# The chunked scan's outputs and states made for two sequences in one group of TensorE products, from the second block on

## The chip, the cores and the metric

One core of a Trainium2 chip. The metric is the device time of one execution in microseconds (us). A core has five engines that run their own instruction lists: PE (TensorE, products), ACT (ScalarE), DVE (VectorE), POOL (GpSimd) and SP (SyncE, which only issues the DMAs here). They wait for one another by semaphores.

## The reference

A gated linear recurrence over 4 sequences of 768 positions, 8 heads, head size 32, state size 16, whose output (3072 tokens of 256 features) goes through two dense networks with 2048 hidden units; float32 throughout.

```python
for c in range(nc):                       # chunks of the sequence
    cum = np.cumsum(log_a[:, :, sl], axis=-1)
    L = np.exp(cum[:, :, :, None] - cum[:, :, None, :]) * causal
    M = np.einsum('bhin,bhjn->bhij', Cc, Bc) * L
    y_intra = np.einsum('bhij,bhjd->bhid', M, xc)
    y_inter = np.einsum('bhin,bhnd->bhid', Cc, state) * np.exp(cum)[:, :, :, None]
    y[:, :, sl] = y_intra + y_inter
    decay_from_j = np.exp(cum[:, :, -1:] - cum)
    Bx = np.einsum('bhjn,bhjd->bhjnd', Bc, xc) * decay_from_j[:, :, :, None, None]
    state = np.exp(np.sum(la, -1))[:, :, None, None] * state + np.sum(Bx, axis=2)
x = y.transpose(0, 2, 1, 3).reshape(3072, 256)
h = x @ moe_w_in
x = (np.maximum(h, 0) + np.log1p(np.exp(-np.abs(h)))) @ moe_w_out
h = x @ moe2_w_in
return np.where(h >= 1, h, np.where(h <= -1, 0, (h + 1) ** 2 / 4)) @ moe2_w_out
```

## The kernel before, in words

The recurrence is cut into blocks of 128 positions: 6 blocks (c) times 4 sequences (b) make 24 units, u = 4c + b. The features of a block, four units side by side, are the 512 tokens of one pass of the dense networks.

Every piece of work is a named job. `program` adds all jobs with an engine, a cost in ns, what they need, the buffers that they take and give back, and for some a due time; `Jobs.order` runs a list scheduler over them once, while the kernel is built, and the code is written out in that order. So each engine's instruction list is fixed by the table of costs and due times, and a change of one job can move others.

The jobs of a unit, in their order:

- `load`, `load_bc` (for two units), `rows`, `dec` (for a block): DMAs that SP issues.
- `decay` (DVE, a scan of 128x1024) makes the decay matrix in a tile `ld`; `cd` (DVE) scales C; `sources` (DVE) scales B.
- `scores` (PE, line 791) makes C times B for two units at once: its four banks of PSUM are the two of the tile `y` (also called `pair`) and two `acc` banks. `weigh` (DVE, line 800, two for a unit) multiplies them into `ld`.
- `out` (PE) makes the unit's features and its state's increment in the tile `y`: 4 products with the old state on 32 rows (line 824), 8 products with x that fill 32 columns each (line 829), and, except in the last block, 4 products for the state (line 836). Each is recorded as two matmuls in the profile.
- `evac` (ACT, line 849) copies the features to `xh`, rounded to the type that PE reads fast; `ready` (DVE, line 858) writes the remainder to `xl`, and for blocks 1 to 4 brings the state `s` forward (line 860). `sm` (ACT) spreads the state for the next block's `out`.

There is one tile `y`, so `out` of a unit waits until `ready` of the unit before it has read it.

The dense networks run in steps: `up` (PE, lines 891 to 893: three products for one of float32, with the high and low parts of features and weights), the nonlinearity `g` (ACT, and DVE in the second network), `g_hi` and `g_lo` (the split of g into high and low part, on ACT, DVE and, for some, POOL, line 930), `down` (PE, line 956). In blocks 0 and 1 a step has 256 tokens (two sequences) and two slices of the hidden size; later it has 512 tokens and one. Weights come as float64 and are turned into a high and a low part by the jobs `w0` to `w3`, `w_hi` and `split_w` on ACT, DVE and POOL.

The tables that matter here, as the scheduler had them: `out` 900 ns (750 in block 0), `evac` 270 ns, `ready` 340 ns, 190 ns more with the state.

Of the kernel before, what the change touches and what calls it, by code (L numbers as in the profile page):

```python
# [12 lines left out]
ALU = mybir.AluOpType  # L13

NB, H, S, D, N = 4, 8, 768, 32, 16
Q = 128
# [154 lines left out]
def place_of(kind, j):  # L171

    return (2 if kind == "i" else 4) + j // 4


def signed(m, kind, j):

    return m == 0 and j < PRELU[kind == "o"]
# [4 lines left out]
    return s < WHOLE  # L183


def on_act(s):

    return NFC * NC <= s < ACT_UNTIL


def program():
# [39 lines left out]
    for u in range(NU):  # L231
# [25 lines left out]
        if b % 2:  # L257
            v = u // 2
            add(
                ("scores", v), PE, 1350, needs=[("load_bc", v)] + (decay + [("decay", u - 1)] if c else [("scores", v - 1)] * v),  # L260
                takes=["y", "acc", "acc"] if c else ["y"] + [("acc", "h")] * 2 if v == 0 else [("h", "acc")] * 4,
                gives=[("load_bc", v)],
            )
        for hg in range(2):
# [10 lines left out]
        needs = [("weigh", u, 0), ("weigh", u, 1)] + ([("out", u - 1)] if u else [])  # L275
        if c > 0:
            needs += [("cd", u), ("sm", u - NB)]
        add(
            ("out", u), PE, 900 if c else 750, needs=needs, takes=["y"],
            gives=[("load", u), ("rows", u) if c else ("part", ("spread", u, 0), 1)] + [("sources", u) if c else ("sources", u, 0)] * (c < NC - 1),  # L280
        )
        needs = [("out", u)]
        if c > 1:
            needs += [("split_w", 0, kind, j) for kind in "io" for j in range(8) if place_of(kind, j) == c]
            needs += [("down", s) for s in range(WHOLE)]
        if c == 1:

            needs += [("w2" if signed(0, kind, SX) else "w3", 0, kind, SX) for kind in "io"]
        due = when(first_step[c, b] - LEAD if c < 2 else min(first_step[c, b] - LEAD, CHUNK * (c - 1) + SPACE * b + SHIFT))
        add(("evac", u), ACT, 270 + 150 * (c == 0), needs=needs)  # L290
        add(
            ("ready", u), DVE, 340 + 190 * (0 < c < NC - 1), due=due, needs=[("evac", u)],
            gives=[("out", u)] + [("dec", c)] * (b == NB - 1 and c > 0),
        )
        if c < NC - 1:
            add(("sm", u), ACT, 500, needs=[("ready", u)] + [("decay", 3, 1)] * (u < NB))


    last_use, first_use = {}, {}
# [26 lines left out]
    for s, (m, c, t0, n, fc, m_fc) in enumerate(steps):  # L326
        pieces = sorted({(fc + i) // 2 for i in range(m_fc)})
        if m == 0:
            needs = [("ready", NB * c + b) for b in range(t0 // Q, (t0 + n) // Q)]
# [96 lines left out]
def tile_kernel(ctx: ExitStack, tc: tile.TileContext, a0, al, bc, ub, w_in, w_out, w2_in, w2_out, out):  # L426
# [380 lines left out]

    emit["copy"] = copy_scores

    def y_t():  # L810

        buf("y", 0)
        return bufs["pair"][:, :, 0:Q], bufs["pair"][:, 0, Q:Q + 64]

    def out_unit(engine, u):
        c, b = divmod(u, NB)
        (y, state), ld = y_t(), ld_t(u)
        x, _, cdt = parts(u)

        if c > 0:  # L820
            for p in range(4):

                r, o = slice(p * 32, p * 32 + 32), p % 2 * 64
                nc.tensor.matmul(  # L824
                    y[o:o + 64, p // 2], sm_t[b][r], cdt[r], start=True, stop=False, skip_group_check=True,
                )
        for h in range(H):
            r = slice(h % 4 * 32, h % 4 * 32 + 32)
            nc.tensor.matmul(  # L829
                y[r, h // 4], x[:, h * 32:h * 32 + 32], ld[:, h, :], start=(c == 0), stop=True, skip_group_check=True,  # L830
            )
        if c < NC - 1:
            bt = flat(bt_t(u))
            for p in range(4):
                r = slice(p * 32, p * 32 + 32)
                nc.tensor.matmul(
                    state[r], bt[:, p * 32:p * 32 + 32], x[:, p * 64:p * 64 + 64], start=False, stop=True,
                    skip_group_check=True,
                )

    emit["out"] = out_unit

    @job
    def evac(engine, u):
        c, b = divmod(u, NB)
        y, state = y_t()
        if b == 0:
            xh[c], xl[c] = (new(f"x{i}{c}", F32R, f"x{i}{c}") for i in "hl")
        nc.scalar.copy(xh[c][:, :, b * Q:(b + 1) * Q], y)  # L849
        if c == 0:  # L850
            nc.scalar.copy(s_t[b], state)

    @job
    def ready(engine, u):
        c, b = divmod(u, NB)
        y, state = y_t()
        hi, lo = (t[:, :, b * Q:(b + 1) * Q] for t in (xh[c], xl[c]))
        nc.vector.tensor_tensor(out=lo, in0=y, in1=hi.bitcast(F32), op=ALU.subtract)  # L858
        if 0 < c < NC - 1:
            nc.vector.scalar_tensor_tensor(  # L860
                out=s_t[b], in0=s_t[b], scalar=mine("dec", c)[0][:, b, Q - 1:Q], in1=state,
                op0=ALU.mult, op1=ALU.add,
            )

    @job
# [220 lines left out]
```

## Time and profile before

| | |
|---|---|
| median of 3 runs | 597.13 us (596.39 to 599.62) |
| the profiled execution | 597.06 us |
| its span, first to last instruction | 595.3 us |
| PE busy | 583.7 us, 98% of the span |
| DVE busy | 469.2 us, 79% |
| ACT busy | 258.6 us, 43% |
| POOL busy | 38.0 us, 6% |
| TensorE's mean granted clock | 1.000 |

A busy engine had an instruction in it; PE's are pipelined, so that its busy share says little of the pace. The pace is read from the starts of successive products.

### The profile page before, as it was taken

To read this page: it belongs to the slowest core of one execution; us is meant where nothing else is said; L and a number is where in the kernel's file an instruction comes from. 1 tells how busy PE (TensorE), PEld (TensorE's weight loads), DVE (VectorE), ACT (ScalarE), POOL (GpSimd) and SP (SyncE) were. 2 spreads that over 40 slices of the span, in tenths; PEclk is the share of its full clock that TensorE was granted. 3 is DMA by queue.
4 is the path that set the end of the run, shared out by engine and by line. 5 is a ranking of instruction groups with operands and counts; after the bars stand their busy time and mean duration, and the time that the engine had idled before them with its cause. 6 is when DMAs were issued, how large, how long until landed. Compare 5 with 4: busy or idle time off the path is not lost.

```text
span 595.3 us, 9221 instructions
## 1 busy us (share of the span) xinstructions
PE 583.7 (98%) x3598; PEld 482.6 (81%) x3598; DVE 469.2 (79%) x789; ACT 258.6 (43%) x469; POOL 38.0 (6%) x28
## 2 busy tenths in 40 slices
PE   7799999999999999999999999999999999999997
PEld 3699989997787778778888888888888888888886
DVE  6899996886756763558998766679899899899895
ACT  5957453443433332236655876653222322322321
POOL 4285300000000000000000000000000000000000
PEclk9999999999999999999999999999999999999999
DMA  7986342522420320005430000000000000000000
GB/s 269 398 303 200 115 138 80 199 90 79 134 70 28 107 72 0 1 1 178 141 107 0 1 1 2 0 35 2 37 0 1 35 2 0 36 0 2 35 1 36
DMA packets 19863, 43.68 MB, mean 73 GB/s; under 512 B 1740, under 2 KB 2316, under 8 KB 19820
## 3 DMA queue, kind: packets, MB, share of 16 engines
q1 hardware_dynamic: 19820, 43.10, 21.2%
q8 instruction: 28, 0.46, 0.3%
q14 instruction: 15, 0.12, 0.1%
HBM read 39.75 MB, written 3.34 MB: 72 GB/s over the span
## 4 chain that ended last, share of the span: by engine, by line
PE 94%; POOL 1%; ACT 1%; DMA 1%; DVE 1%; issue 1%; SPq 0%; ACTq 0%
PE acc L956 43%; PE h L891 11%; PE h L893 10%; PE h L892 10%; PE y L829 2%; PE acc L891 2%; PE acc L892 2%; PE acc L893 2%; PE z L892 2%; PE z L893 2%; PE z L891 2%; PE acc L944 2%; PE y L791 2%; POOL gl L930 1%; PE y L824 1%; DMA st<-in_w_in_dram 1%
## 5 line engine op out<-in xcount | busy, mean ns | idle before, releaser
L956 PE MATMUL acc<-gh,woh 128*128 128x512 f32 (+1 forms) x424 | 152.4, 367 | 0.0
L956 PE MATMUL acc<-gh,wol 128*128 128x512 f32 (+1 forms) x424 | 150.6, 363 | 0.0
L930 DVE TENSOR_TENSOR gl<-g,gh 128x512 fp32r<-128x512 f32 x182 | 125.9, 692 | 21.7 <-ACT gh L501 10.8
L891 PE MATMUL h<-xh,wih 128*128 128x512 f32 (+1 forms) x332 | 120.3, 362 | 0.5 <-ACT xh L849 0.5
L893 PE MATMUL h<-xl,wih 128*128 128x512 f32 (+1 forms) x332 | 118.2, 356 | 0.0
L892 PE MATMUL h<-xh,wil 128*128 128x512 f32 (+1 forms) x332 | 118.1, 356 | 0.0
L956 PE MATMUL acc<-gl,woh 128*128 128x512 f32 (+1 forms) x424 | 115.5, 363 | 0.8 <-POOL gl L930 0.8
L503 DVE CAST gh<-g 128x512 fp32r<-128x512 f32 x121 | 52.6, 435 | 52.1 <-ACT g L915 43.6
L956 PEld LDWEIGHTS acc<-gh,woh 128*128 128x128 f32 x424 | 79.9, 188 | 14.8 <-issue 0.9
L956 PEld LDWEIGHTS acc<-gh,wol 128*128 128x128 f32 x424 | 80.0, 189 | 12.2
L902 ACT ACTIVATE t<-h 128x512 f32<-128x512 f32 x63 | 37.7, 599 | 112.1 <-PE h L893 112.1
L956 PEld LDWEIGHTS acc<-gl,woh 128*128 128x128 f32 x424 | 74.4, 189 | 13.6 <-POOL gl L930 1.0
L891 PEld LDWEIGHTS h<-xh,wih 128*128 128x128 f32 x332 | 62.6, 189 | 12.4 <-issue 2.2
L893 PEld LDWEIGHTS h<-xl,wih 128*128 128x128 f32 x332 | 62.6, 189 | 9.1 <-DVE xl L858 0.2
L892 PEld LDWEIGHTS h<-xh,wil 128*128 128x128 f32 x332 | 62.7, 189 | 8.7
L915 ACT ACTIVATE g<-h 128x512 f32<-128x512 f32 x55 | 32.9, 597 | 74.8 <-PE h L893 67.4
L921 DVE SCALAR_TENSOR_TENSOR t<-t 128x512 f32<-128x512 f32 x72 | 49.6, 690 | 6.0 <-ACT t L902 5.8
L501 ACT CAST gh<-g 128x512 fp32r<-128x512 f32 x65 | 40.4, 621 | 21.9 <-DVE g L922 16.8
L755 DVE TENSOR_TENSOR_SCAN ld<-ld,eye_t 128x1024 f32<-128x1024 f32 x20 | 45.5, 2281 | 0.2 <-DMA ld<-clip_z 0.2
L922 DVE TENSOR_TENSOR g<-h,t 128x512 f32<-128x512 f32 x63 | 43.5, 691 | 2.2
L915 ACT ACTIVATE g<-acc 128x512 f32<-128x512 f32 x27 | 16.1, 598 | 36.1 <-PE acc L893 36.0
L891 PE MATMUL acc<-xh,wih 128*128 128x512 f32 (+1 forms) x66 | 23.2, 352 | 0.0
(147 smaller groups left out, 660.5 us busy)
## 6 DMA issues: line engine op xcount, KB each, us to landing
ld<-clip_z SPq DMA_DIRECT2D x20, 512.0 KB, 4.2
st<-in_w_in_dram SPq DMA_DIRECT2D x15, 512.0 KB, 6.9
st<-in_w_out_dram SPq DMA_DIRECT2D x15, 512.0 KB, 5.1
u<-in_ub_dram SPq DMA_DIRECT2D x24, 256.0 KB, 3.7
bc<-in_bc_dram SPq DMA_DIRECT2D x12, 384.0 KB, 3.5
out_dram<-dec SPq DMA_DIRECT2D x6, 256.0 KB, 3.0
dec<-clip_p SPq DMA_DIRECT2D x5, 256.0 KB
out_dram<-bc SPq DMA_DIRECT2D x5, 256.0 KB, 2.2
```

The lines of the kernel that those rows point to most:

```text
L501: nc.scalar.copy(out, in_)
L503: engines[engine].tensor_copy(out, in_)
L755: nc.vector.tensor_tensor_scan(t, t, eye_t, 0.0, ALU.mult, ALU.add)
L891: nc.tensor.matmul(o, wh, xh[c][:, k, t0:t0 + n], start=(k == 0), stop=False)
L892: nc.tensor.matmul(o, wl, xh[c][:, k, t0:t0 + n], start=False, stop=False)
L893: nc.tensor.matmul(o, wh, xl[c][:, k, t0:t0 + n], start=False, stop=(k == 1))
L902: nc.scalar.activation(out=t, in_=ph, func=AF.Relu, bias=0.5, scale=0.5)
L915: nc.scalar.activation(out=g, in_=ph, func=AF.Softplus)
L921: nc.vector.scalar_tensor_tensor(out=t, in0=t, scalar=1.0, in1=t, op0=ALU.min, op1=ALU.mult)
L922: nc.vector.tensor_tensor(out=g, in0=ph, in1=t, op=ALU.max)
L930: engines[engine].tensor_tensor(out=mine("g_lo", s)[0], in0=mine("g", s)[0], in1=mine("g_hi", s)[0].bitcast(F32), op=ALU.subtract)
L956: nc.tensor.matmul(acc_t(s, e), w, g[:, j * n:(j + 1) * n], start=(begins(e, j) and g is gh and i == 0), stop=(fc + j == NFC - 1 and g is ...
```

## The change

In block 0 nothing changes in the jobs. From block 1 on `out`, `evac` and `ready` are made for two sequences at a time, at the odd unit: `out` puts the 8 products of both with the old state first, then the 16 with x, then the 8 for the states. The features of the two lie side by side in the tile `y` (columns 0 to 127 and 128 to 255 of each bank, the states' increments behind them), one `evac` copies 2x256 columns, one `ready` subtracts 2x256 columns and then brings both states forward with an instruction each. `ready_of` names the job that a later job waits for. The scheduler's costs are: `out` 2200 ns for the pair, `evac` 490, `ready` 610 and 380 more with the states, `scores` 1270 where it was 1350.

```diff
+def ready_of(u):
+
+    return u if u < NB else u | 1
...
-                ("scores", v), PE, 1350, needs=[("load_bc", v)] + (decay + [("decay", u - 1)] if c else [("scores", v - 1)] * v),
+                ("scores", v), PE, 1270, needs=[("load_bc", v)] + (decay + [("decay", u - 1)] if c else [("scores", v - 1)] * v),
...
+        both = [u] if c == 0 else [u - 1, u]
+        if c == 0 or b % 2:
+
+            needs = [("weigh", i, hg) for i in both for hg in range(2)] + ([("out", both[0] - 1)] if u else [])
+            if c > 0:
+                needs += [(kind, i - NB * (kind == "sm")) for i in both for kind in ("cd", "sm")]
+            add(
+                ("out", u), PE, 2200 if c else 750, needs=needs, takes=["y"],
...
+            add(("evac", u), ACT, 490 if c else 420, needs=needs)
+            add(
+                ("ready", u), DVE, 610 + 380 * (c < NC - 1) if c else 340, due=due, needs=[("evac", u)],
...
+            add(("sm", u), ACT, 500, needs=[("ready", ready_of(u))] + [("decay", 3, 1)] * (u < NB))
...
+    def y_t(u):
 
         buf("y", 0)
-        return bufs["pair"][:, :, 0:Q], bufs["pair"][:, 0, Q:Q + 64]
+        i = u % 2 if u >= NB else 0
+        return bufs["pair"][:, :, i * Q:i * Q + Q], bufs["pair"][:, 0, 256 + i * 64:320 + i * 64]
...
+        units = [u] if c == 0 else [u - 1, u]
 
         if c > 0:
-            for p in range(4):
-
-                r, o = slice(p * 32, p * 32 + 32), p % 2 * 64
+            for i in units:
+                y, cdt = y_t(i)[0], parts(i)[2]
+                for p in range(4):
+
+                    r, o = slice(p * 32, p * 32 + 32), p % 2 * 64
+                    nc.tensor.matmul(
+                        y[o:o + 64, p // 2], sm_t[i % NB][r], cdt[r], start=(i == units[0]), stop=False, skip_group_check=True,
+                    )
+        for i in units:
+            y, x, ld = y_t(i)[0], parts(i)[0], ld_t(i)
+            for h in range(H):
+                r = slice(h % 4 * 32, h % 4 * 32 + 32)
                 nc.tensor.matmul(
...
+        for i in units if c < NC - 1 else []:
+            state, x, bt = y_t(i)[1], parts(i)[0], flat(bt_t(i))
...
+    def columns_of(c, b):
+
+        buf("y", 0)
+        n, o = (Q, b * Q) if c == 0 else (2 * Q, b * Q - Q)
+        return [bufs["pair"][:, :, 0:n]] + [t[c][:, :, o:o + n] for t in (xh, xl)]
...
-        nc.scalar.copy(xh[c][:, :, b * Q:(b + 1) * Q], y)
+        y, hi, _ = columns_of(c, b)
+        nc.scalar.copy(hi, y)
...
+        y, hi, lo = columns_of(c, b)
         nc.vector.tensor_tensor(out=lo, in0=y, in1=hi.bitcast(F32), op=ALU.subtract)
-        if 0 < c < NC - 1:
+        for i in (u - 1, u) if 0 < c < NC - 1 else ():
+            s = s_t[i % NB]
             nc.vector.scalar_tensor_tensor(
```

The change of the jobs moves others. Three places follow, in each engine's own list; line numbers of the changed kernel are some 9 to 19 higher for the same code.

PE, the first pair of block 1 (units 4 and 5, whose operands are the tiles `u_130` and `u_131`). Before, unit 4, then a `down` step of block 0:

```order
L956 MATMUL acc_238<-gl,woh_98 128x256 x4
L824 MATMUL y<-u_130,sm_141 64x128 x4
L829 MATMUL y<-ld_123,u_130 32x128 x8
L836 MATMUL y<-u_130,bt_258 32x64 x4
L956 MATMUL acc_216<-gh,woh_97 128x256
```

and, two `down` steps later, unit 5, with the first `up` step of block 1 right behind it:

```order
L956 MATMUL acc_216<-gl,woh_98 128x256 x4
L824 MATMUL y<-u_131,sm_142 64x128 x4
L829 MATMUL y<-ld_119,u_131 32x128 x8
L836 MATMUL y<-u_131,bt_294 32x64 x4
L891 MATMUL h_160<-xh_961,wih_75 128x256
```

In the changed kernel, both at the place of unit 4:

```order
L974 MATMUL acc_238<-gl,woh_98 128x256 x4
L835 MATMUL y<-u_130,sm_141 64x128 x4
L835 MATMUL y<-u_131,sm_142 64x128 x4
L842 MATMUL y<-ld_123,u_130 32x128 x8
L842 MATMUL y<-ld_119,u_131 32x128 x8
L849 MATMUL y<-u_130,bt_258 32x64 x4
L849 MATMUL y<-u_131,bt_294 32x64 x4
L974 MATMUL acc_216<-gh,woh_97 128x256
```

The pair stands where unit 4 stood, and both `down` steps now lie between it and the first `up` step that reads its features (line 909 there).

DVE, towards the end of the first network's weights (`wil_90` is the low part of the last piece of the first weight matrix, `wih_82` its high part, the two rows `gl<-g,gh` are the jobs `g_lo` of steps 9 and 10). Before:

```order
L930 TENSOR_TENSOR gl<-g,gh 128x512
L599 SCALAR_TENSOR_TENSOR w_669<-st_139,w_669 128x512
L587 SCALAR_TENSOR_TENSOR w_749<-w_749,t 128x512
L563 TENSOR_SCALAR w_749<-st_137 128x512
L599 SCALAR_TENSOR_TENSOR w_749<-st_136,w_749 128x512
L609 TENSOR_TENSOR wil_90<-w_669,wih_82 128x512
L930 TENSOR_TENSOR gl<-g,gh 128x512
```

In the changed kernel:

```order
L948 TENSOR_TENSOR gl<-g,gh 128x512
L608 SCALAR_TENSOR_TENSOR w_669<-st_139,w_669 128x512
L596 SCALAR_TENSOR_TENSOR w_763<-w_763,t 128x512
L512 CAST wih_82<-w_669 128x512
L608 SCALAR_TENSOR_TENSOR w_763<-st_136,w_763 128x512
L618 TENSOR_TENSOR wil_90<-w_669,wih_82 128x512
L948 TENSOR_TENSOR gl<-g,gh 128x512
```

The high part `wih_82` is made by DVE itself now, in place of a piece that ACT makes instead (`w_749<-st_137`), so that `wil_90` needs nothing of ACT any more. From the first row of DVE's list to the one ahead of the second `g_lo` shown, DVE has in sum one subtraction of 128x512 more than before had up to the row ahead of `wil_90`.

DVE again, between the pair of units 6 and 7 and that of units 8 and 9 (`ld_119` is the matrix of unit 9, `xl_981` holds the remainders of block 1, `s_68` and `s_145` are the states of sequences 2 and 3). Before, the two units of the pair are weighed one behind the other, and the `ready` of unit 7 comes after that:

```order
L800 TENSOR_TENSOR ld_123<-acc_216,ld_123 128x512
L800 TENSOR_TENSOR ld_122<-y,ld_122 128x512
L800 TENSOR_TENSOR ld_123<-acc_214,ld_123 128x512
L930 TENSOR_TENSOR gl<-g,gh 128x512
L763 TENSOR_TENSOR bt_258<-u_132,ld_119 128x128
L858 TENSOR_TENSOR xl_962<-y,xh_961 128x2x128
L860 SCALAR_TENSOR_TENSOR s_145<-s_145,dec_134,y 128x64
```

In the changed kernel:

```order
L809 TENSOR_TENSOR ld_119<-acc_238,ld_119 128x512
L876 TENSOR_TENSOR xl_981<-y,xh_980 128x2x256
L879 SCALAR_TENSOR_TENSOR s_68<-s_68,dec_134,y 128x64
L879 SCALAR_TENSOR_TENSOR s_145<-s_145,dec_134,y 128x64
L809 TENSOR_TENSOR ld_119<-acc_214,ld_119 128x512
L512 CAST gh<-g 128x512
L948 TENSOR_TENSOR gl<-g,gh 128x512
```

The last of the four products by which the pair of units 8 and 9 is weighed (the second `ld_119` row) now stands behind the `ready` of the pair of units 6 and 7, which cannot start before their `out` and `evac` are done. In PE's list of the changed kernel 36 products of 256 columns (two `down` steps and an `up` step) lie between the two `out`.

Two smaller moves: on ACT, ahead of the first softplus, the spreading of a state (line 869) changes places with a conversion of weights (line 567); and one `g_lo` of block 0, that of step 15, goes from POOL to DVE.

## Rows read from the trace of the kernel before

**Rows 1.** The page's head: the span of the profiled execution.

```profile
span 595.3 us, 9221 instructions
```

**Rows 2.** Waits of PE from 25 us on: us in total, times, longest.

```profile
PE acc L956 <- POOL gl L930: 0.8, 1, 0.8
PE h L891 <- ACT xh L849: 0.5, 1, 0.5
```

**Rows 3.** Busy time by stretch: us; PE, PEld, DVE, ACT, POOL, clock, DMA.

```profile
25.00:60.00 35.00, 34.20 (x255) 32.34 (x254) 33.17 (x51) 24.79 (x46) 23.63 (x3) 1.00 0.79 269
...
76.00:125.00 49.00, 49.00 (x554) 44.99 (x555) 41.08 (x69) 21.03 (x46) 0.00 (x0) 1.00 0.42 141
```

**Rows 4.** Timeline of PE around one unit's `out`: start us, us, instruction, matmuls.

```profile
146.56 0.39 PE L892 MATMUL acc<-xh,wil 128*128 128x512 f32 x1
146.79 0.39 PE L893 MATMUL acc<-xl,wih 128*128 128x512 f32 x1
147.10 0.45 PE L824 MATMUL y<-u,sm 32*64 32x128 f32 x8
147.48 0.64 PE L829 MATMUL y<-ld,u 128*32 128x128 f32 x16
147.94 0.29 PE L836 MATMUL y<-u,bt 128*32 128x64 f32 x8
148.17 0.50 PE L956 MATMUL acc<-gh,woh 128*128 128x512 f32 x1
148.51 0.40 PE L956 MATMUL acc<-gh,wol 128*128 128x512 f32 x1
```

**Rows 5.** Groups by line and shape, 66 to 266 us: `out` in blocks 1 to 5.

```profile
L824 PE MATMUL y<-u,sm 32*64 32x128 f32 x160 | 9.0, 293 | 0.0
```

**Rows 6.** Timeline of PE, `out` of the last unit.

```profile
263.79 0.39 PE L893 MATMUL acc<-xl,wih 128*128 128x512 f32 x1
...
265.39 0.39 PE L956 MATMUL acc<-gh,wol 128*128 128x512 f32 x1
```

**Rows 7.** Timeline of PE, inside `scores`.

```profile
151.65 0.38 PE L791 MATMUL y<-bc 32*128 32x256 f32 x2
...
151.86 0.38 PE L791 MATMUL y<-bc 32*128 32x256 f32 x2
```

**Rows 8.** Timeline of PE, the two places at which it waits.

```profile
59.39 0.74 PE L956 MATMUL acc<-gl,woh 128*128 128x256 f32 x4 [0.80 <-POOL gl L930]
75.89 0.39 PE L891 MATMUL h<-xh,wih 128*128 128x256 f32 x1 [0.49 <-ACT xh L849]
```

**Rows 9.** Timeline of POOL: two subtractions of the same size (start, us).

```profile
50.83 8.51 POOL L930 TENSOR_TENSOR gl<-g,gh 128x512 fp32r<-128x512 f32 x1 [7.36 <-ACT gh L501]
60.31 1.30 POOL L930 TENSOR_TENSOR gl<-g,gh 128x512 fp32r<-128x512 f32 x1 [0.97 <-PE acc L956]
```

**Rows 10.** Timeline of DVE and of ACT at the same time.

```profile
60.51 1.65 DVE L609 TENSOR_TENSOR wil<-w,wih 128x512 fp32r<-128x512 f32 x1 [2.30 <-ACT wih L501]
59.37 0.60 ACT L915 ACTIVATE g<-h 128x512 f32<-128x512 f32 x1 [1.19 <-POOL gl L930]
59.87 0.61 ACT L501 CAST wih<-w 128x512 fp32r<-128x512 f32 x1
```

**Rows 11.** Groups by line and shape, 60 to 270 us, DVE and ACT: mean ns.

```profile
L800 DVE TENSOR_TENSOR ld<-acc,ld 128x512 f32<-128x512 f32 x20 | 13.6, 680 | 0.0
L860 DVE SCALAR_TENSOR_TENSOR s<-s,dec,y 128x64 f32<-128x64 f32 x16 | 4.3, 271 | 0.0
L501 ACT CAST xh<-acc 128x512 fp32r<-128x512 f32 x4 | 2.1, 588 | 1.0 <-PE acc L956 1.0
```

**Rows 12.** Timeline of ACT around the first softplus.

```profile
21.69 0.54 ACT L869 ACTIVATE sm<-s,of_one 128x32 f32<-128x32 f32 x2
...
24.39 0.70 ACT L567 ACTIVATE w<-raw 128x512 f32<-128x512 f32 x1
```

More of the change, by code (lines that the diff above doesn't have):

```diff
@@ L274, in program @@
                 add(("weigh", u, hg), DVE, 600, needs=weighed + [("weigh", u, 0)] * hg + [("scores", u // 2)], gives=bank)
[L275 to L294, printed above, removed]
+        both = [u] if c == 0 else [u - 1, u]
[5 more added lines that the diff above has]
+                ("out", u), PE, 2200 if c else 750, needs=needs, takes=["y"],
+                gives=[("load", i) for i in both] + [("rows", i) if c else ("part", ("spread", u, 0), 1) for i in both]
+                + [("sources", i) if c else ("sources", u, 0) for i in both] * (c < NC - 1),
+            )
+            needs = [("out", u)]
+            if c > 1:
+                needs += [("split_w", 0, kind, j) for kind in "io" for j in range(8) if place_of(kind, j) == c]
+                needs += [("down", s) for s in range(WHOLE)]
+            if c == 1:
+                needs += [("w2" if signed(0, kind, SX) else "w3", 0, kind, SX) for kind in "io"]
+            due = when(first_step[c, b] - LEAD if c < 2 else min(first_step[c, b] - LEAD, CHUNK * (c - 1) + SPACE * b + SHIFT))
+            add(("evac", u), ACT, 490 if c else 420, needs=needs)
+            add(
+                ("ready", u), DVE, 610 + 380 * (c < NC - 1) if c else 340, due=due, needs=[("evac", u)],
+                gives=[("out", u)] + [("dec", c)] * (b == NB - 1 and c > 0),
+            )
@@ L295, in program @@
         if c < NC - 1:
-            add(("sm", u), ACT, 500, needs=[("ready", u)] + [("decay", 3, 1)] * (u < NB))
+            add(("sm", u), ACT, 500, needs=[("ready", ready_of(u))] + [("decay", 3, 1)] * (u < NB))
     last_use, first_use = {}, {}
@@ L328, in program @@
         if m == 0:
-            needs = [("ready", NB * c + b) for b in range(t0 // Q, (t0 + n) // Q)]
+            needs = [("ready", ready_of(NB * c + b)) for b in range(t0 // Q, (t0 + n) // Q)]
         else:
@@ L845, in evac @@
         c, b = divmod(u, NB)
-        y, state = y_t()
-        if b == 0:
+        if c not in xh:
             xh[c], xl[c] = (new(f"x{i}{c}", F32R, f"x{i}{c}") for i in "hl")
-        nc.scalar.copy(xh[c][:, :, b * Q:(b + 1) * Q], y)
+        y, hi, _ = columns_of(c, b)
+        nc.scalar.copy(hi, y)
         if c == 0:
-            nc.scalar.copy(s_t[b], state)
+            nc.scalar.copy(s_t[b], y_t(u)[1])
     @job
@@ L855, in ready @@
         c, b = divmod(u, NB)
-        y, state = y_t()
-        hi, lo = (t[:, :, b * Q:(b + 1) * Q] for t in (xh[c], xl[c]))
+        y, hi, lo = columns_of(c, b)
         nc.vector.tensor_tensor(out=lo, in0=y, in1=hi.bitcast(F32), op=ALU.subtract)
-        if 0 < c < NC - 1:
+        for i in (u - 1, u) if 0 < c < NC - 1 else ():
+            s = s_t[i % NB]
             nc.vector.scalar_tensor_tensor(
-                out=s_t[b], in0=s_t[b], scalar=mine("dec", c)[0][:, b, Q - 1:Q], in1=state,
-                op0=ALU.mult, op1=ALU.add,
+                out=s, in0=s, scalar=mine("dec", c)[0][:, i % NB, Q - 1:Q], in1=y_t(i)[1], op0=ALU.mult, op1=ALU.add,
             )
```

13 lines of the change are left out of this document (2 added, 11 removed).

## The prediction, made before the changed kernel ran

> **What bounds the kernel now.** I read the page's first part, then the waits of PE, then the stretches, then PE's timeline at single places. PE is busy nearly all the time, but that says little, since its products overlap. Two other things say that PE sets the end. From 25 us on it waits twice in 570 us: 0.8 us for POOL and 0.5 us for ACT [rows 2]. And its products start at an even step: 0.23 us from one 512-column product to the next (146.56 to 146.79) [rows 4]. So after 25 us the time is the sum of what PE's list holds, and a change counts only if it alters that sum or makes PE wait. DVE is the second limit: 33.17 of 35 us busy between 25 and 60 us, 41.08 of 49 us between 76 and 125 us [rows 3]. What is added or reordered there has little cover.
>
> **PE: one group for two.** One `out` costs more than its products. From the L893 that starts at 146.79 to the second L956 at 148.51 are 1.72 us [rows 4]; two ordinary steps would take 0.46, so the unit takes 1.26 us. What of this is streaming? Inside `scores` four recorded matmuls of 256 columns take 0.21 us (151.65 to 151.86; the other two are those of the acc bank) [rows 7], so two streams run side by side and a recorded column costs 0.21 ns. By that measure L824 (8x128 columns) needs 0.21 us, L829 (16x128) 0.43 and L836 (8x64) 0.11, in sum 0.75 us, an estimate. The other 0.51 us lie at the changes of form, read off the starts [rows 4]: 0.08 ahead of L824 (0.31 where 0.23 is usual), 0.17 behind it (0.38 to L829, less 0.21), 0.03 behind L829, 0.12 behind L836, 0.11 on the first L956. In the last block, without L836, the same reckoning gives 1.60 less 0.46, 1.14 us, for 0.64 of streaming [rows 6]: 0.50 again.
>
> A pair goes through the same forms once where two units go twice. If the second unit's products follow the first's at the streaming pace, a pair costs 1.50 + 0.51 = 2.01 us where two units cost 2.52. The 160 recorded L824 are 20 units of 8 [rows 5], so ten pairs are made and 10 x 0.51 = 5.1 us go. L829 shows 0.03 more than streaming, which may belong to each unit and not to the change of form; I take 0.48 a pair, **4.8 us**. Bounds: 5.1 if all of it is shared, 0 if every unit starts afresh inside the group.
>
> **PE: the wait behind unit 5.** The first `up` of block 1 stands right behind unit 5's `out` and waits 0.49 us for its features [rows 8]. In the new list two `down` steps stand between. They have 24 products of 256 columns, about 24 x 0.115 = 2.8 us at half the step of 512 columns. Against this stand the copy of 0.59 us on ACT and the subtraction of 0.68 on DVE [rows 11], 1.3 us, behind at most one subtraction or half a scan that DVE is in. The wait goes: **-0.5 us**. Bounds -0.5 and 0.
>
> **DVE: one subtraction ahead of POOL's.** PE's other wait, 0.80 us at 59.39, is for POOL's L930 [rows 8]. That instruction takes 8.51 us, from 50.83 to 59.34, where the next of the same size takes 1.30 [rows 9]. It ends when DVE is at rest: DVE waits 2.30 us until 60.51 for `wih` from ACT, and ACT is held at L915 until 59.37 by that same POOL instruction [rows 10]. So POOL gets through once DVE's list stops. In the new list DVE makes `wih_82` itself and goes on with `wil_90`, and stops only at the `g_lo` behind it; it has one subtraction more ahead of its stop, 0.68 us at the price of an equal one [rows 11]. POOL then ends 0.7 us later, and PE, which gets to that place on an unchanged list, waits 1.5 us instead of 0.8: **+0.7 us**. Bounds: -0.8 if DVE pauses earlier for some other job and lets POOL in, +1.7 if DVE gets there a further 1 us late, which is what one more POOL subtraction held against it would cost (60.51 took 1.65 where 0.68 is usual) [rows 10].
>
> The Trainium skill, page "GPSIMD Engine Reference", section "Key points", says that POOL shares its SBUF interfaces with VectorE and contends with DVE instructions that have two SBUF inputs or run in a 2-port mode. The trace agrees with it: 8.51 us against 1.30 [rows 9]. By that rule the term is +0.7; if a slow POOL instruction were simply 8.51 us long, it would be 0.
>
> **What costs nothing.** ACT has ten copies fewer and DVE ten subtractions fewer; both beside PE. Ahead of the first softplus a conversion of 0.70 takes the place of a spreading of 0.54 [rows 12]: +0.1 or so in a stretch where PE has idle time anyway; I set it to 0, bounds -0.2 and +0.3. The new waits of a pair I set to 0 for this reason. Between the `out` of units 6 and 7 and that of 8 and 9 PE has 36 products of 256 columns, about 36 x 0.115 = 4.1 us. The chain that must fit in is copy 0.59, subtraction 0.68, two states at 0.27, one product of DVE at 0.68 [rows 11]: 2.5 us. That leaves 1.6 us for handing over and for what DVE is in. DVE's busy share there, 84% [rows 3], is the cover; if it is gone, the first bound is some 1 us for each of the three pairs behind in that stretch, 3 us. Later blocks have more room.
>
> **Sum.** -4.8 - 0.5 + 0.7 = -4.6 us. The profiled execution took 597.06 us for a span of 595.3 [rows 1], and is within 0.1 us of the median, 597.13. So 597.06 - 4.6 = 592.5 us.
>
> **Rivals.**
> Rival 1, the pair waits. The pair needs four weighed tiles where the first unit needed two, and there is one tile `y`. For it speaks that DVE is 84% to 95% busy up to 125 us [rows 3] and that a weighing now stands behind `ready`. Against it the 1.6 us worked out above. Price: 2 to 5 us, so 594.5 to 597.5.
> Rival 2, nothing is shared inside the group: the second unit's products start afresh, as the first ones do. For it: no row shows two units back to back. Against it: in `scores` the pace is even from the second round on [rows 7]. It gives half, 2.4 us, or nothing: 594.9 to 597.3.
> Rival 3, slower: in every pair PE stands until the later unit's two weighings, 2 x 0.68 us [rows 11], are done, because the scheduler put the pair where the first unit stood. Ten times 1.4 us less 4.6 is +9 us: 606. Against it: in block 1 the first pair's products are all weighed well ahead in DVE's list. It would take 0.8 us in each pair to end 0.5% above (600.1). The same would come from DVE falling behind by 8 us between 25 and 76 us, where it has 1.8 us to spare up to 60 us [rows 3]; but the new list gives it one instruction more, not twelve.
>
> **How the numbers follow.** My forecast, 590.7 to 594.1, has 68%; the low end is -5.1 - 0.5 - 0.8 (590.7). A still larger gain has 3%. Rival 1 has 14%, rival 2 10%, rival 3 5%. To hold 8 in 10 the range goes up into rivals 1 and 2, to 596.0, where half of the pair's gain is left (-2.4), the wait at 75.89 is gone, and POOL's costs its upper bound of 1.7. About 0.5%, 3 us, is what a measurement of this kernel can tell from no change; so faster means below 594.1, slower above 600.1. Faster 0.72 (the forecast, the larger gain, and a little of rival 1), same 0.22, slower 0.06.
>
> **What would show it.** The pair's group on PE: from the product ahead to the second one behind, less two ordinary steps, 2.0 us; 2.5 means rival 2. PE's waits from 25 us on: the one at the first `up` of block 1 gone, the one for POOL near 1.5 us, and no wait at an L835. A wait there for DVE would be rival 1, several of them rival 3. From 275 us on the two traces should differ by a constant. The prediction is wrong if the groups shrink as forecast and the time comes back as waits of PE between 60 and 125 us, or if the order of the weights' jobs makes PE wait between 25 and 58 us, where before it did not.

## The result and the profile after

The changed kernel takes 590.18 us (median of 4 runs, 589.86 to 590.43); the kernel before took 597.24 us beside it (4 runs, 596.39 to 599.62). The ratio is 0.9875, 95% interval 0.9846 to 0.9904. The prediction was 592.5 us with a range of 590.7 to 596.0: the direction was right, the gain is half as large again, and the time is 0.5 us below the range. The profiled execution took 590.31 us, 6.75 less than that of before. From 25 us on the granted clock was 0.99 or 1.00 in every trace used below, so no difference there comes from it.

The head of the page after, which answers to [rows 1], and its busy times:

```profile
span 588.6 us, 9187 instructions
...
PE 578.5 (98%) x3598; PEld 482.6 (82%) x3598; DVE 469.5 (80%) x779; ACT 256.8 (44%) x460; POOL 17.5 (3%) x27
```

POOL's busy time is the figure to notice: 17.5 us for work that took 38.0 us before, though it has only one subtraction less. Two subtractions of weights, which end long before PE's wait for POOL, make 10.4 us of the difference (4.7 where they took 15.1), and the subtraction that PE waited for makes 7.1.

The list of PE's waits from 25 us on, which answers to [rows 2], is empty: both waits of before are gone, where the prediction expected one of them to grow. Next, PE's timeline around one pair's `out`, which answers to [rows 4], and around a pair of the last block, which answers to [rows 6]:

```profile
141.69 0.39 PE L911 MATMUL h<-xl,wih 128*128 128x512 f32 x1
142.00 0.67 PE L835 MATMUL y<-u,sm 32*64 32x128 f32 x16
142.60 1.08 PE L842 MATMUL y<-ld,u 128*32 128x128 f32 x32
143.50 0.41 PE L849 MATMUL y<-u,bt 128*32 128x64 f32 x16
143.83 0.50 PE L974 MATMUL acc<-gh,woh 128*128 128x512 f32 x1
144.17 0.40 PE L974 MATMUL acc<-gh,wol 128*128 128x512 f32 x1
...
242.16 0.39 PE L911 MATMUL h<-xl,wih 128*128 128x512 f32 x1
...
244.43 0.40 PE L974 MATMUL acc<-gh,wol 128*128 128x512 f32 x1
```

From 141.69 to 144.17 are 2.48 us; less two ordinary steps (0.46) the pair costs 2.02, where 2.01 was forecast and two units took 2.52. In the last block it is 244.43 - 242.16 - 0.46 = 1.81, where two units took 2 x 1.14 = 2.28. All ten groups show these two figures within 0.02, each less two ordinary steps of its own surroundings (0.23 us for 512 columns, 0.12 for 256).

The two places at which PE waited before, in the timeline of PE after (they answer to [rows 8]):

```profile
58.21 0.28 PE L974 MATMUL acc<-gh,wol 128*128 128x256 f32 x1
58.33 0.64 PE L974 MATMUL acc<-gl,woh 128*128 128x256 f32 x4
58.81 0.28 PE L974 MATMUL acc<-gh,woh 128*128 128x256 f32 x1
...
73.30 0.64 PE L974 MATMUL acc<-gl,woh 128*128 128x256 f32 x4
73.78 0.28 PE L909 MATMUL h<-xh,wih 128*128 128x256 f32 x1
```

At 58.33 the four products of the low half follow their predecessor by the ordinary 0.12 us, and the first `up` of block 1 follows a `down` step without a pause. The rows of before that stand around the two waits:

```profile
58.32 0.28 PE L956 MATMUL acc<-gh,wol 128*128 128x256 f32 x1
...
59.97 0.28 PE L956 MATMUL acc<-gh,woh 128*128 128x256 f32 x1
...
75.10 0.29 PE L836 MATMUL y<-u,bt 128*32 128x64 f32 x8
...
76.57 0.28 PE L891 MATMUL h<-xh,wih 128*128 128x256 f32 x1
...
85.58 0.29 PE L836 MATMUL y<-u,bt 128*32 128x64 f32 x8
...
86.26 0.28 PE L891 MATMUL h<-xh,wih 128*128 128x256 f32 x1
```

Before, the predecessor started at 58.32, the four at 59.39 [rows 8] and the next at 59.97: 0.95 us late at the start, and 0.58 instead of 0.48 for the four. So a wait that the list of waits shows with 0.80 had cost 1.05. The same holds behind unit 5. From its L836 at 75.10 to the fourth product of the `up` step at 76.57 are 1.47 us; behind unit 8, where nothing waits, the same stretch (85.58 to 86.26) takes 0.68. So that wait had cost 0.79, where the list shows 0.49: the first product came 0.56 late, and the second and third step behind it took 0.24 and 0.22 where 0.12 is usual.

**Where the 6.75 us come from.** Take the same product of PE in both traces, at the starts of the `up` steps. The changed kernel is ahead by 0.11 us from 26 to 56 us (a shorter head), by 1.16 from 60 us on (56.04 against 55.93, then 61.41 against 60.25): the wait for POOL. It is ahead by 3.83 at the end of block 1, by 5.90 at the end of block 3, by 6.91 at the end of block 4, during which the last pairs are made, and by 6.91 still at the last `up` (585.47 against 578.56). The step from 1.16 to 6.91 is 5.75 us. It holds the wait behind unit 5, 0.79, and ten groups, 4.96 us; the groups' own lengths give the same (8 x 0.50 and 2 x 0.47). Behind PE's last product the changed kernel needs 0.2 us more (584.46 to 588.6, against 591.37 to 595.3). In sum 0.11 + 1.05 + 0.79 + 4.96 - 0.2 = 6.7.

**Why POOL was early.** The timelines of POOL and DVE after, which answer to [rows 9] and [rows 10], and ACT's at the same time:

```profile
26.49 4.74 POOL L618 TENSOR_TENSOR wol<-w,woh 128x512 fp32r<-128x512 f32 x2 [9.47 <-ACT woh L510]
51.54 1.38 POOL L948 TENSOR_TENSOR gl<-g,gh 128x512 fp32r<-128x512 f32 x1 [20.31 <-ACT gh L510]
...
51.10 0.67 DVE L596 SCALAR_TENSOR_TENSOR w<-w,t 128x512 uint32<-128x512 uint32 x1
51.73 1.47 DVE L572 TENSOR_SCALAR w<-st 128x512 f32<-128x512 f32 x1
...
51.73 0.77 ACT L584 ACTIVATE t<-st,low_bias 128x512 uint32<-128x512 uint32 x1 [0.27 <-DMA st<-in_w_in_dram]
```

The subtraction that took 8.51 us took 1.38, and it ended (52.92) inside DVE's L572, which took 1.47 us where the same form takes 0.41 elsewhere. L572 is the job `w0` of piece 7 of the first weight matrix (the experiments call it the scaled or masked product). The scheduler had put it on ACT before and puts it on DVE now, and in exchange the rounding (`w_hi`) of piece 6 has gone from DVE to ACT. The row of ACT shows what L572 met: the piece had only just landed, and ACT, waiting for it, started at the same 51.73. That is 0.03 us behind DVE's usual step (51.10 + 0.60).

### The profile page after: what moved, and what is told of

Its sections match the earlier page's. It is cut to its first block, busy times and chain, and to the rows that moved or that the text cites. A ratio compares the mean times of both kernels' runs of the same rounds, so it can differ in the third digit from the quotient of the medians.

```text
span 588.6 us, 9187 instructions
## 1 busy us (share of the span) xinstructions
PE 578.5 (98%) x3598; PEld 482.6 (82%) x3598; DVE 469.5 (80%) x779; ACT 256.8 (44%) x460; POOL 17.5 (3%) x27
## 4 chain that ended last, share of the span: by engine, by line
PE 95%; DMA 3%; DVE 0%; SPq 0%; issue 0%; ACT 0%
PE acc L974 44%; PE h L909 11%; PE h L911 11%; PE h L910 11%; PE acc L909 2%; PE acc L910 2%; PE acc L911 2%; DMA bc<-in_bc_dram 2%; PE z L909 2%; PE z L911 2%; PE z L910 2%; PE acc L962 2%; PE y L800 2%; PE y L842 2%; DMA st<-in_w_out_dram 1%; PE y L835 1%
## 5 line engine op out<-in xcount | busy, mean ns | idle before, releaser
L948 DVE TENSOR_TENSOR gl<-g,gh 128x512 fp32r<-128x512 f32 x183 | 127.3, 697 | 18.3 <-ACT gh L510 7.1
L512 DVE CAST gh<-g 128x512 fp32r<-128x512 f32 x118 | 50.4, 427 | 53.3 <-ACT g L933 45.1
L510 ACT CAST gh<-g 128x512 fp32r<-128x512 f32 x68 | 42.2, 621 | 19.2 <-DVE g L940 16.8
```

What stands on the lines that cost most here:

```text
L510: nc.scalar.copy(out, in_)
L512: engines[engine].tensor_copy(out, in_)
L948: engines[engine].tensor_tensor(out=mine("g_lo", s)[0], in0=mine("g", s)[0], in1=mine("g_hi", s)[0].bitcast(F32), op=ALU.subtract)
```

## The experiments

Two questions: what does a pair save on PE, and what lets POOL's subtraction in? For the first, theory A says that each change of form is paid once instead of twice. For the second, theory B says that POOL's subtraction runs when DVE stops; its rivals say that POOL was early because its earlier jobs were (they ended at 31 us instead of 43), or because of the two exchanged jobs as such. Offsets below are starts of the same product against the kernel before, so that a longer or shorter head of one execution drops out; they come from one profiled execution of each kernel. The times of the runs are medians, and the kernel before, which ran beside each of them, had medians of 596.44 to 596.66 us, so it is the ratios that can be compared.

### unit_by_unit

The products of a group, unit by unit, in the changed kernel:

```diff
-        if c > 0:
-            for i in units:
-                y, cdt = y_t(i)[0], parts(i)[2]
-                for p in range(4):
...
         for i in units:
-            y, x, ld = y_t(i)[0], parts(i)[0], ld_t(i)
+            (y, state), (x, _, cdt), ld = y_t(i), parts(i), ld_t(i)
+            for p in range(4 if c > 0 else 0):
...
             for h in range(H):
...
-        for i in units if c < NC - 1 else []:
-            state, x, bt = y_t(i)[1], parts(i)[0], flat(bt_t(i))
-            for p in range(4):
+            for p in range(4 if c < NC - 1 else 0):
...
```

> The changed kernel, with the products inside each group of two put back unit by unit: old-state, score and new-state products of the first unit, then those of the second. The list of jobs, the evacuation and all else stay as changed. Theory A (the saving of 0.5 us a pair is that each change of form is paid once in the group instead of twice): the group goes from 2.02 to about 2.5 us, PE's starts fall behind those of the changed kernel by 0.5 us at each of the ten pairs, in sum 5 us; time near 595.2 us, ratio to before about 0.997. Rival (the saving comes from one evacuation, fewer waits and fewer jobs for two units): the group stays near 2.0 us and the time near 590.2, ratio 0.988.

592.66 us (4 runs, 592.33 to 594.36), ratio to before 0.9928 (0.9901 to 0.9955). PE's timeline at the same group, 2 us later than in the changed kernel:

```profile
143.89 0.39 PE L906 MATMUL h<-xl,wih 128*128 128x512 f32 x1
144.21 0.45 PE L834 MATMUL y<-u,sm 32*64 32x128 f32 x8
144.59 0.64 PE L839 MATMUL y<-ld,u 128*32 128x128 f32 x16
145.05 0.29 PE L844 MATMUL y<-u,bt 128*32 128x64 f32 x8
145.27 0.45 PE L834 MATMUL y<-u,sm 32*64 32x128 f32 x8
145.65 0.64 PE L839 MATMUL y<-ld,u 128*32 128x128 f32 x16
146.11 0.29 PE L844 MATMUL y<-u,bt 128*32 128x64 f32 x8
146.33 0.50 PE L969 MATMUL acc<-gh,woh 128*128 128x512 f32 x1
146.67 0.40 PE L969 MATMUL acc<-gh,wol 128*128 128x512 f32 x1
```

The group takes 146.67 - 143.89 - 0.46 = 2.32 us: neither 2.02 nor 2.5. With the streaming of the prediction (0.11 for eight of 64 columns) the rows say why. The second unit's start costs 0.22 - 0.11 = 0.11 (145.05 to 145.27), where two units apart pay 0.11 + 0.11 to leave the first (rows L844 and L969) and 0.08 to enter the second. So of the 0.50 us a pair, 0.20 come from the two units standing side by side, and 0.30 from the sorting of their products. Over ten groups PE falls behind the changed kernel by 3.0 us, as 10 x 0.30 asks. Theory A holds with a correction, since the group is 0.2 us shorter than it forecast: the price depends on which form follows which. The rival forecast 2.0 us for the group and falls, since the evacuations and jobs are those of the changed kernel.

### states_shared_only

Only the old-state products of both first; score and new-state products unit by unit:

```diff
         for i in units:
             y, x, ld = y_t(i)[0], parts(i)[0], ld_t(i)
+            state, bt = y_t(i)[1], flat(bt_t(i)) if c < NC - 1 else None
             for h in range(H):
...
-        for i in units if c < NC - 1 else []:
-            state, x, bt = y_t(i)[1], parts(i)[0], flat(bt_t(i))
-            for p in range(4):
+            for p in range(4 if c < NC - 1 else 0):
...
```

> The changed kernel; in each group the old-state products of both units still come first, but the score and the new-state products go unit by unit. So entering the group and the change behind the old-state products are shared, and the changes between score and new-state products (0.03 and 0.12 us by the starts in the kernel before) are paid twice in the nine pairs that make new states. Theory A with the price of each change as read before: group 2.2 to 2.3 us with new states, still 1.8 in the last block, where the order is the same as in the changed kernel but for nothing; sum +1.4 to +2.5 us against the changed kernel, 591.6 to 592.7. Rival (what costs is only entering and leaving the group, not the changes within): group stays at 2.0, time 590.2.

589.64 us (4 runs, 589.11 to 592.96), ratio 0.9891 (0.9855 to 0.9926). PE's timeline, from the execution of 592.96 us, whose granted clock was 0.93 over the first 25 us and 1.00 here:

```profile
144.17 0.39 PE L910 MATMUL h<-xl,wih 128*128 128x512 f32 x1
...
145.55 0.29 PE L848 MATMUL y<-u,bt 128*32 128x64 f32 x8
145.66 0.62 PE L843 MATMUL y<-ld,u 128*32 128x128 f32 x16
146.09 0.29 PE L848 MATMUL y<-u,bt 128*32 128x64 f32 x8
146.32 0.50 PE L973 MATMUL acc<-gh,woh 128*128 128x512 f32 x1
146.66 0.40 PE L973 MATMUL acc<-gh,wol 128*128 128x512 f32 x1
```

146.66 - 144.17 - 0.46 = 2.03 us: the group costs what it costs in the changed kernel, and the forecast of 2.2 to 2.3 was wrong. (The pairs that make new states are eight, not the nine of the expectation.) The rival's figure came, but not its reason: that changes within the group cost nothing is refuted by `unit_by_unit`, where they cost 0.30 us. From 145.55 to 145.66 are 0.11 us, the streaming of eight products of 64 columns and nothing more. So the 0.12 us "behind L836" of the prediction are not paid behind L836 as such, but where 128*128 follows. The forms to count are the blocks of the array in the rows (32*64, 128*32, 128*128), not the lines. Entering 32*64 from 128*128 costs 0.08, 32*64 to 128*32 0.17, 128*32 to 32*64 0.11, 128*32 to 128*128 0.22, and a change of operand within 128*32 0.00 to 0.03. The Trainium skill, page "TensorEngine Tiling (Array Packing)", section "Key Properties", says that a change of the tiling mode, and not of the tile alone, drains TensorE. The two runs agree, and the prices are theirs.

### two_jobs_back and cost_1350_kept

First, the changed kernel with the two exchanged jobs back on the engines of before:

```diff
+    moved = {("w0", 0, "i", 7): ACT, ("w_hi", 0, "i", 6): DVE}
+    order = [(name, moved.get(name, engine), slots) for name, engine, slots in order]
```

> The changed kernel with two jobs of the first block on the engines that they had before: the scaled product of piece 7 of the input weights (1 of 8) on ACT, and the rounding of piece 6 on DVE. Theory B (POOL's subtraction at 51 us ended after 1.4 us because DVE, which had just been given the job on piece 7, stood there and waited for that piece's transfer): DVE does not stop there now; POOL's subtraction gets long again (6 to 9 us), PE waits for it 0.5 to 1.6 us near 59 us, and the time is 0.7 to 1.6 us above the changed kernel's, 590.9 to 591.8. Rival C (POOL was early for another reason, such as that its two earlier jobs were done by 31 us instead of 43): POOL's subtraction takes under 2 us, PE has no wait at 59 us, time 590.2.

591.21 us (4 runs, 590.05 to 591.45), ratio 0.9901 (0.9877 to 0.9926). The list of PE's waits, and POOL's timeline:

```profile
PE acc L976 <- POOL gl L950: 0.9, 1, 0.9
```

```profile
51.35 7.81 POOL L950 TENSOR_TENSOR gl<-g,gh 128x512 fp32r<-128x512 f32 x1 [20.30 <-ACT gh L510]
```

POOL is slow again and PE waits, although POOL's two earlier jobs ended at 31 us as in the changed kernel (that rival falls). The lead over the kernel before goes from 0.29 to 0.19 at this place, where in the changed kernel it goes from 0.11 to 1.16: by these two traces the exchange is worth 1.15 us. The median is 1.0 us above the changed kernel's, but the intervals of the two ratios overlap, so the times alone do not show it.

Second, the changed kernel with the scheduler's cost of `scores` left at 1350, so that the same work stands in another order:

```diff
-                ("scores", v), PE, 1270, needs=[("load_bc", v)] + (decay + [("decay", u - 1)] if c else [("scores", v - 1)] * v),
+                ("scores", v), PE, 1350, needs=[("load_bc", v)] + (decay + [("decay", u - 1)] if c else [("scores", v - 1)] * v),
```

> The changed kernel with the list-maker's cost of the score products left at 1350 as before (1270 in the change): the same work, only another order of the jobs. It measures what the order alone moves. Theory: PE has no waits to lose from 25 us on, so a different order can only add waits of the size seen before, 0 to 1.6 us: 590.2 to 591.8. Rival (the gain beyond the group's comes by luck of one order only): PE shows both waits of before again, +1.3 us or more, 591.5 or above.

591.20 us (9 runs, 590.90 to 594.97), ratio 0.9924 (0.9902 to 0.9946). POOL's timeline, and DVE's at the same time:

```profile
51.15 8.49 POOL L948 TENSOR_TENSOR gl<-g,gh 128x512 fp32r<-128x512 f32 x1 [20.88 <-ACT gh L510]
...
52.60 0.42 DVE L512 CAST wih<-w 128x512 fp32r<-128x512 f32 x1
```

POOL's subtraction takes 8.49 us and PE's wait for it is the 0.8 us of before. A wait of 0.4 us for ACT comes at 35 us. The wait behind unit 5 is gone here too, so of the rival's two waits one came back: that term does not hang on the order, and the 1.05 us of POOL do. DVE's row says why. The rounding of piece 6 (L512) stands where the changed kernel has the product L572, so with the old cost of `scores` the scheduler does not exchange the two jobs, although `out`, `evac` and `ready` are made for two here as well. The 1.05 us come with the line of the change that writes 1270 for 1350, and not with the grouping itself. (Given 1270 in the kernel before, its scheduler makes the same exchange in its list; that kernel was not run.)

### before_jobs_exchanged and before_g_lo_on_dve

Now the other way round, the kernel before with the exchange alone:

```diff
+    moved = {("w0", 0, "i", 7): DVE, ("w_hi", 0, "i", 6): ACT}
+    order = [(name, moved.get(name, engine), slots) for name, engine, slots in order]
```

> The kernel before, with the two jobs on the engines that the changed kernel gives them: the scaled product of piece 7 of the input weights on DVE, the rounding of piece 6 on ACT; nothing else. Theory B (POOL's subtraction runs when DVE's list has a stop, however short, and not before): if the new row of DVE at 52.3 us, or the subtraction behind it that now needs ACT's rounding, shows a stop of some hundredths of a us, POOL's subtraction of 8.5 us ends within 1.4 us of that stop, PE's wait of 0.8 us at 59 us is gone, and PE runs 1.05 us earlier behind it: 595.4 us by the runs of before of the first call (596.46 median). If DVE shows no stop, all stays: 596.5. Rival C (POOL is early where its earlier jobs are done early, or its length has nothing to do with a stop of DVE): a stop of DVE near 53 us with POOL's subtraction still ending at 59 us, 596.5.

595.37 us (9 runs, 594.65 to 598.92; before 596.66 over 20 runs), ratio 0.9973 (0.9951 to 0.9994). Timelines of POOL, DVE and ACT:

```profile
50.30 3.65 POOL L932 TENSOR_TENSOR gl<-g,gh 128x512 fp32r<-128x512 f32 x1 [7.37 <-ACT gh L501]
...
52.09 0.69 DVE L601 SCALAR_TENSOR_TENSOR w<-st,w 128x512 uint32<-128x512 uint32 x1
52.70 1.80 DVE L611 TENSOR_TENSOR wil<-w,wih 128x512 fp32r<-128x512 f32 x1
...
52.05 0.61 ACT L501 CAST wih<-w 128x512 fp32r<-128x512 f32 x1
```

The wait for POOL is gone and PE is 1.05 us earlier behind it (0.54 to 1.59). Theory B was right on the time and wrong on what is to be seen: DVE's L611 shows no stop, since 52.70 is its usual step behind 52.09. It takes 1.80 us, though, and POOL ends inside it, at 53.95. What stands out at L611 is that its input from ACT was ready at 52.66, 0.04 us ahead of its turn. That gives theory B2: POOL gets in where DVE's next input is ready only as its turn comes, or later.

The price of the wait by itself, in the kernel before, with POOL's subtraction (`g_lo` of step 12) put on DVE:

```diff
+    moved = {("g_lo", 12): DVE}
```

> The kernel before, with POOL's subtraction at 50.8 us (the low half of the gated product of one step) put on DVE, where it costs about 0.6 us of DVE's time. It prices PE's wait for POOL by itself. Theory: the wait of 0.80 us at 59.39 is gone and PE runs 0.8 to 1.05 us earlier from there, 595.4 to 595.7 us; POOL has only the two subtractions of 1.3 us left in that stretch. Rival: DVE, 0.6 us later, makes PE wait at the same place or the next step instead: 596.0 to 597.

595.34 us (10 runs, 594.96 to 598.12), ratio 0.9977 (0.9960 to 0.9995). The wait is gone, and the offset goes from -0.94 to 0.11: 1.05 us again. From 30 us on PE has one wait left, the 0.5 us for ACT behind unit 5, and the rival falls.

### rounding_early and rounding_late

Both build on the kernel before and tell B2 from the two jobs as such (rival D). The first has both exchanged jobs, and ACT's rounding one place earlier (the diff is against `before_jobs_exchanged`):

```diff
     moved = {("w0", 0, "i", 7): DVE, ("w_hi", 0, "i", 6): ACT}
     order = [(name, moved.get(name, engine), slots) for name, engine, slots in order]
+    early = [j for j in order if j[0] == ("w_hi", 0, "i", 6)]
+    order = [j for j in order if j not in early]
+    at = [j[0] for j in order].index(("g", 9))
+    order = order[:at] + early + order[at:]
```

> The kernel before with the two jobs exchanged as in the run before_jobs_exchanged, and ACT's rounding of piece 6 one place earlier on ACT, ahead of the gating that waits for PE: the same work on the same engines, one order of two jobs on ACT other. In before_jobs_exchanged ACT's rounding ended at 52.66 and DVE's subtraction that reads it started at its usual step at 52.70; POOL's subtraction came in there. Theory B2 (POOL comes in where the input of DVE's next instruction is ready only as that instruction's turn comes, or later; a visible stop is not needed): the rounding now ends near 51.9, 0.8 us ahead of DVE's turn, DVE has nothing to wait for, POOL's subtraction is long again, 7 to 9 us, and PE's wait of about 0.8 us at 59 us is back; 596.4 to 596.7 us, as before. Rival D (it is the two jobs on these engines themselves, such as the masked product on DVE, that let POOL in): POOL's subtraction stays at 3 to 4 us, no wait, 595.4.

596.80 us (10 runs, 596.07 to 597.47; before 596.44), ratio 0.9998 (0.9982 to 1.0014). The list of PE's waits, and the timelines of POOL, DVE and ACT:

```profile
PE acc L962 <- POOL gl L936: 0.8, 1, 0.8
```

```profile
50.64 8.50 POOL L936 TENSOR_TENSOR gl<-g,gh 128x512 fp32r<-128x512 f32 x1 [7.36 <-ACT gh L501]
...
53.04 0.68 DVE L615 TENSOR_TENSOR wil<-w,wih 128x512 fp32r<-128x512 f32 x1
...
51.62 0.62 ACT L501 CAST wih<-w 128x512 fp32r<-128x512 f32 x1 [0.39 <-DVE w L605]
```

The same jobs on the same engines; only ACT's rounding is done at 52.24, 0.8 us ahead of DVE's turn at 53.04. POOL takes 8.50 us, and the wait of 0.8 us is back. Rival D falls.

The second has the rounding alone on ACT, behind the scaled product:

```diff
-    moved = {("w0", 0, "i", 7): DVE, ("w_hi", 0, "i", 6): ACT}
+    moved = {("w_hi", 0, "i", 6): ACT}
```

> The kernel before with only the rounding of piece 6 moved from DVE to ACT; the scaled product of piece 7 stays on ACT, ahead of it. ACT then rounds near 52.6 to 53.2 us, DVE is 0.3 us less busy and comes to the subtraction that reads it near 52.9. Theory B2: DVE stops there for 0.2 to 0.4 us, POOL's subtraction comes in and ends by 54.3 (under 4 us long), PE's wait at 59 us is gone: 595.4 to 595.6 us. Rival D (the masked product of piece 7 on DVE is what lets POOL in): POOL's subtraction is long, the wait stays: 596.4 to 596.7.

595.46 us (10 runs, 594.98 to 596.74), ratio 0.9974 (0.9959 to 0.9988). DVE and POOL:

```profile
50.31 2.69 POOL L932 TENSOR_TENSOR gl<-g,gh 128x512 fp32r<-128x512 f32 x1 [7.38 <-ACT gh L501]
...
51.17 0.68 DVE L589 SCALAR_TENSOR_TENSOR w<-w,t 128x512 uint32<-128x512 uint32 x1
51.89 1.66 DVE L601 SCALAR_TENSOR_TENSOR w<-st,w 128x512 uint32<-128x512 uint32 x1
```

The wait is gone (offset 0.53 to 1.58), as B2 forecast, but at another place. With the rounding gone from DVE's list, L601 follows directly on the instruction whose result it reads. That one ends at 51.85, so L601 starts at 51.89 instead of 51.77. DVE waits 0.12 us for itself, and POOL comes in there, not at the subtraction behind it.

### last_block_in_one, beside changed_again

By these prices the last block's four units, which make no states, should stand in one group (the lines cut at the end give the larger group its costs and its columns of `y`):

```diff
-    return u if u < NB else u | 1
+    return u if u < NB else u | (3 if u >= NU - NB else 1)
...
+def group_of(c, u):
+
+    return [u] if c == 0 else list(range(u - 3 if c == NC - 1 else u - 1, u + 1))
...
-        both = [u] if c == 0 else [u - 1, u]
-        if c == 0 or b % 2:
+        both = group_of(c, u)
+        if ready_of(u) == u:
...
```

> The changed kernel, with the last block's four units in one group instead of two pairs (they make no states, so the product tile has room): 32 old-state products, 64 score products, one evacuation, one subtraction. By the price of the changes of form that the runs so far show (0.08 into the old-state products, 0.17 from these to the score products, 0.23 out) one set goes: 0.5 us less than the changed kernel, group 1.14 x 4 less 3 x 0.5, about 3.1 us where two pairs take 3.2 and four units of before 4.6; 589.7 us if the changed kernel takes 590.2. Rival: the group stands until the fourth unit's weighings, or the first product behind it waits for the larger evacuation: PE shows a wait near 250 us, and the time is 590.2 or above.

> The changed kernel as it is, beside the others on the same chip. 590.2 us, ratio 0.9875 to 0.990. It also shows whether POOL's early subtraction at 51 us comes again in another execution: by theory B DVE's stop for piece 7's transfer was 0.03 us, which a later execution need not have, and then the wait of 0.8 us at 59 us is back and the time is 591.2.

589.30 us (5 runs, 588.68 to 589.89), ratio 0.9854 (0.9833 to 0.9876); the changed kernel beside it 590.12 us (5 runs, 589.30 to 590.70), ratio 0.9869 (0.9847 to 0.9890). PE's timeline of the group of four:

```profile
255.39 0.62 PE L979 MATMUL acc<-gl,woh 128*128 128x512 f32 x2
255.94 1.10 PE L840 MATMUL y<-u,sm 32*64 32x128 f32 x32
256.97 1.95 PE L847 MATMUL y<-ld,u 128*32 128x128 f32 x64
...
259.19 0.40 PE L915 MATMUL h<-xh,wil 128*128 128x512 f32 x1
```

From the second of the two at 255.39 (255.62) to 259.19 less 0.46 are 3.11 us, as forecast. Two pairs take 2 x 1.81 = 3.62 (the 3.2 of the expectation is a slip), so the group is 0.5 us shorter. From 60 us to the end PE gains 0.56 us more than in `changed_again`, and it has no wait from 25 us on. The traces show the half microsecond; the two intervals overlap, so the times alone do not.

`changed_again` did not lose the early POOL: its subtraction took 1.38 us, and ACT's and DVE's rows on piece 7 stand side by side again (51.49, behind a wait for the transfer, and 51.51). In the three runs where piece 7 had landed in time (`unit_by_unit`, `states_shared_only`, `last_block_in_one`) the subtraction took 2.33 to 2.34 us: POOL came in at DVE's next stop, 0.43 to 0.44 us for ACT's rounding of piece 6. The exchange gave POOL two openings.

## Why the prediction was half right

**PE, one group for two: right, and 0.2 us short.** 2.01 us a pair was forecast and 2.02 measured. The term was -4.8 us because 0.03 a pair were left out as belonging to each unit; the ten groups give 5.0. Rival 2 (each unit starts afresh) is what `unit_by_unit` builds: half of it is true there, 2.32 us. The mechanism was named right. Where the prices lie was not: the 0.12 and 0.11 us on both sides of the end of `out` are one change, out of 128*32.

**PE, the wait behind unit 5: right, and mis-sized.** -0.5 was forecast from the list of waits and 0.79 measured by the starts. It is gone also where the order is another (`cost_1350_kept`). That the two `down` steps in between are what covers it was argued, not tested by itself.

**DVE, one subtraction ahead of POOL's: the step that failed.** The forecast was +0.7 us, PE's wait growing to 1.5; it fell to nothing, 1.05 us were saved, and the term was off by 1.75 us. The reasoning "POOL gets through once DVE's list stops" held, with one correction: in `before_jobs_exchanged` no stop is to be seen, and an input that came 0.04 us ahead of its turn did the same. What failed is the next sentence, that DVE "stops only at the `g_lo` behind it". It was read from the end of the list, where the moved subtraction stands. Some ten places earlier two jobs had exchanged engines, and the one now on DVE reads a piece of weights that lands just then. That exchange came with the new cost of `scores`, which the prediction did not price. For the change it was luck: nothing in it aimed at POOL. The bound of -0.8 named the case ("if DVE pauses earlier for some other job") and was still 0.25 too small: the list of waits counts 0.80 from the recorded end of the product ahead (58.32 + 0.28), which lies 0.16 behind the next product's ordinary start, and leaves out that the first products after a wait are slower; the starts give 1.05. The other wait was 0.29 too small in the same way. So the low end of the range, 590.7, could not hold the time. The rule of the Trainium skill that was weighed there (page "GPSIMD Engine Reference", section "Key points") speaks of contention on shared interfaces. The runs agree and are sharper: 7.81 to 8.51 us where DVE first stops some 7 us after POOL's start, 1.38 to 3.65 where POOL gets in earlier.

**What costs nothing: right.** No wait at an `out`, none for a pair's features; rival 1 and rival 3 did not come. The head was 0.1 us shorter, the end behind PE 0.2 longer.

By terms, forecast to measured: -4.8 to -5.0, -0.5 to -0.79, +0.7 to -1.05, head 0 to -0.11, end 0 to +0.2: -4.6 to -6.7.

**What stays open.** Where between 0.04 us ahead (POOL gets in) and 0.26 us ahead (the kernel before, where DVE's L599 at 52.64 reads what its own L587 ended at 52.38, and POOL does not) the limit lies was not measured; that a stop too short for the record lies behind the 0.04 is argued, not shown.

## What to carry to other kernels

Where PE sets the end, count the changes of the array's block form between neighbouring products, and sort products by form across units: here each full round of forms cost 0.5 us, and a change of operand within a form at most 0.03. When a new order of jobs is predicted, go through the whole list from where the waiting instruction becomes ready, not only its end: one exchange of two small jobs, which the diff shows only as another cost of `scores`, was worth 1.05 us here. So a cost in a scheduler's table is a change of the kernel, to be tried by itself. And price a wait by the starts of the same product on both sides of it, far enough behind that the usual step is back, not by the length that the list of waits gives.

## What the runs showed of the hardware

By these rows a POOL subtraction of 128x512 makes no headway beside a DVE list without a stop. It ended 1.1 to 1.3 us after the first moment at which DVE had nothing ready, be that 0.2 us after its own start (the changed kernel) or 7.4 (the kernel before), and with DVE at rest at its start it took 1.30 [rows 9]. A stop of 0.12 us, in which DVE waited for its own previous result, was enough (`rounding_late`), and so was an input that came 0.04 us ahead of DVE's turn (`before_jobs_exchanged`). DVE paid for it once: the instruction at which POOL got in took 1.26 to 1.80 us where its form took 0.41 to 0.69 elsewhere.

On PE a change between the block forms 128*128, 32*64 and 128*32 cost 0.08 to 0.22 us, and a change of operand within 128*32 0.00 to 0.03.
